# GpSimd takes layer-norm work, attention products are pre-added to two chunks, and the projections are re-ordered, in a fused attention and gated-MLP kernel

## Chip, cores and metric

The kernel runs on one core of a Trainium2 chip. The metric is the device time of that core in microseconds (us), the median of several executions. Every number below is such a time or comes from the profile of one execution. In the profile PE is TensorE, PEld its weight loads, DVE VectorE, ACT ScalarE, POOL GpSimd and SP SyncE, whose queue issues most transfers. "L371" is line 371 of the program. The changed kernel has one more line early on and three more in the middle, so L370 of before is L371 of after, L423 is L424, L545 is L548, L550 is L553, L576 is L579, and L607 is L610.

## The reference

```python
# S = 2048 tokens, D = 640, 32 heads of 20, F = 1536; bf16 inputs and outputs
xn  = layernorm(x)
q, k, v = split(xn @ wqkv)
# each token attends to 8 keys: itself and those 2, 4, ... 14 tokens back
logits = einsum("bhsd,bhswd->bhsw", q, k[gathered]) * 20 ** -0.5      # masked before token 0
attn   = softmax(logits)
o      = einsum("bhsw,bhswd->bhsd", attn, v[gathered])
out    = x + o @ wo + ((xn @ w_gate) * (xn @ w_up)) @ w_down
```

## The kernel before

A helper records every operation in program order and works out the semaphore waits from what each one reads and writes. Each engine then executes its own operations **in that recorded order**. An operation that waits holds up everything behind it on its engine: in the changed kernel's profile a copy that needs none of them stands behind 13.0 us of GpSimd's operations, and ScalarE stands 17.0 us for that copy.

Layer norm works on 16 tiles of 128 tokens. VectorE makes the statistics and the normalised tile. From tile 4 on, a transposing DMA writes the tile into `XNT`, which all projections read:

```python
def ln_apply(t):
    # ... cut
    op("dve", lambda e: e.reciprocal(rstd, sd), ...)
    op("dve", lambda e: e.tensor_scalar(xs, x, mv[:, 0:1], rstd, op0=ALU.subtract, op1=ALU.mult), ...)
    if t >= NTP:                                   # NTP = 4
        o = XNT[:, :, t * TS:(t + 1) * TS]
        op("sp", lambda e: e.dma_start_transpose(o, xs), ...)
```

Tokens are handled in two halves of 1024 (h = 0, 1), and in four blocks of 512 (j = 0 to 3) for the matmuls. The second half's keys need the last 14 keys of the first half, which GpSimd copies. This copy is the *seam*:

```python
def k_seam():
    o, i = KH[1][:, :, 0:PAD], KH[0][:, :, HS:HS + PAD]
    op("pool", lambda e: e.tensor_copy(o, i), r=[i], w=[o], name="kseam")
```

The logits are made without batched matmuls. VectorE multiplies q by shifted k for two offsets at a time (a *pair*; 4 pairs in each half). It works on five chunks of 128 channels: 3 into a slot of a ring (`SL`) and 2 into `TMP`. It then adds `TMP` to two of the three. TensorE sums what remains over the head channels with a 0/1 matrix, chunk by chunk:

```python
NKC = 3; NSL = 3
return [
    (..., prod(kept, 0, NKC)),              # 128 x 6144
    (..., prod(tmp, NKC, NCH)),             # 128 x 4096
    (..., lambda: op("dve", lambda e: e.tensor_tensor(a, a, b, ALU.add), ...)),   # 128 x 4096, 5 chunks -> 3
]
```

After the softmax, 16 copies for each half bring the weights into place (`ATB`), half of them issued on the SP queue and half on ScalarE's queue. Then eight *value products* of 256 tokens each follow on VectorE (`pv_steps`: a multiply of 128 x 10240, then three adds; the last add writes `VO`).

All other TensorE work is kept in a list in a fixed order: second-half q/k projections, v projections, gate and up matmuls, down projections. The generator keeps two running estimates, `t_pe` and `t_dve`. Each time it records a VectorE step it hands out TensorE work until `t_pe` has caught up:

```python
for i, (m, j, which) in enumerate([(m, j, which) for m in range(NCH) for j in (2, 3) for which in (0, 1)]):
    fill.append((1.08, lambda which=which, m=m, j=j: proj(which, m, j)))
# ... cut: v projections; then gate/up of blocks 0, 1; down of 0; gate/up 2; down 1; gate/up 3; down 2, 3

def run_fill(until, upto=None):
    # ... cut
        if it[0] == "dn":                 # a down-projection tile; it[1] = value product that it needs
            if pv_done[0] <= it[1]:
                return
    # ... cut

def tail(t, nb):       # one half (320 columns) of a down-projection tile: 12 matmuls with WD,
    # ... cut          # 5 with WO and VO, then the residual add FOUT on VectorE
```

Of the kernel before, what the change touches and what calls it, by code (L numbers as in the profile page):

```python
# [5 lines left out]
FP16 = mybir.dt.float16  # L6
ACT = mybir.ActivationFunctionType
ALU = mybir.AluOpType
# [3 lines left out]
NCH = 5  # L12
# [4 lines left out]
W = 8  # L17
# [11 lines left out]
HS = S // 2  # L29
SB = 256  # L30
NSB = HS // SB
# [181 lines left out]
def build_kernel(nc, A_x, A_wqkv, A_wo, B_x, B_w_gate, B_w_up, B_w_down, out):  # L213
    K = Sched(nc)
    op = K.op

    place = [16512]

    def sb(name, shape, dtype=BF16, at=None):
        n = mybir.dt.size(dtype)  # L220
        for s in shape[1:]:
            n *= s
        n = (n + 63) // 64 * 64
        if at is None:
            at = place[0]
            place[0] += n
        assert at + n <= 229344, (name, at + n)
        return K.sbuf(name, shape, dtype, at)
# [1 line left out]
    WG = sb("WG", [128, NCH, F])  # L230
    WU = sb("WU", [128, NCH, F])
    a_pr = place[0]
    NKC = 3
    NSL = 3
    WD = sb("WD", [128, NF, D], at=a_pr)
    WO = sb("WO", [128, NCH, D], at=a_pr + NF * D * 2)
    SL = [sb(f"SL{s}", [128, 2, NKC, HS], FP16) for s in range(NSL)]
    PVB = sb("PVB", [128, NCH, W, SB], FP16, at=place[0] - 2 * NKC * HS * 2)
    TMP = sb("TMP", [128, 2, NCH - NKC, HS], FP16)
    XNT = sb("XNT", [128, NCH, S])  # L240
    VO = sb("VO", [128, NCH, VP + S])
# [20 lines left out]
    NTP = 4  # L262
# [19 lines left out]
    def dma(o, i, r=(), w=(), name="", eng="sp", group=None):  # L282
        return op(eng, lambda e: e.dma_start(o, i), r=r, w=w, dma=True, name=name, group=group)  # L283
# [7 lines left out]
       r=[IDENT[:]], w=[IDENT[:]], name="ident")  # L291
# [3 lines left out]
       r=[G[:]], w=[G[:]], name="g1")  # L295
    op("pool", lambda e: e.affine_select(G[:], G[:], pattern=[[-4, H]], compare_op=ALU.is_ge,
                                         fill=0.0, base=0, channel_multiplier=1),
       r=[G[:]], w=[G[:]], name="g2")
# [3 lines left out]
    def x_load(t, eng="sp"):  # L302
        dma(XST[:, t % NXS, :], xhbm[t * TS:(t + 1) * TS, :], w=[XST[:, t % NXS, :]], name=f"xld{t}", eng=eng)
# [22 lines left out]
    def late_loads():  # L326
        wqkv_load(2)
        for T, src in ((WG, B_w_gate), (WU, B_w_up)):
            dma(T[:], src.rearrange("(c p) n -> p c n", p=128), w=[T[:]], name="ld_w")

    def down_loads():
        dma(WD[:], B_w_down.rearrange("(c p) n -> p c n", p=128), w=[WD[:]], name="ld_wd")

    def out_loads():
        dma(WO[:], A_wo.rearrange("(i m) n -> i m n", m=NCH), w=[WO[:]], name="ld_wo")
# [28 lines left out]
    def ln_apply(t):  # L364
        if t >= NT:
            return
        x, xs, mv = XST[:, t % NXS, :], XNS[:, t % NXN, :], MV[:, t, 0:2]
        sd, rstd = SD[:, t, 0:1], SD[:, t, 1:2]
        op("dve", lambda e: e.reciprocal(rstd, sd), r=[("sd", t)], w=[("rstd", t)], name=f"rstd{t}")  # L369
        op("dve", lambda e: e.tensor_scalar(xs, x, mv[:, 0:1], rstd, op0=ALU.subtract, op1=ALU.mult),  # L370
           r=[x, mv, ("rstd", t)], w=[xs], name=f"lnap{t}")  # L371
        if t >= NTP:
            o = XNT[:, :, t * TS:(t + 1) * TS]
            op("sp", lambda e: e.dma_start_transpose(o, xs), r=[xs], w=[o], dma=True, name=f"xT{t}")
        if t + 8 < NT:
            x_load(t + 8)
        elif t == NT - 1:
            late_loads()
# [26 lines left out]
    bank_ring = list(range(6))  # L405

    def bank():
        b = bank_ring.pop(0)
        bank_ring.append(b)
        return b  # L410
# [46 lines left out]
    def qk_steps(h, p, s):  # L457
        kept, tmp = SL[s], TMP
        kp = KH[h][:, 0, 0:1].ap[0]

        def prod(o, c0, c1):
            q = QH[h][:, c0:c1, :]
            k = KH[h][:, c0:c1, 4 * p:4 * p + HS + 2]
            kw = bass.AP(k.tensor, k.offset, [kp, [2, 2], [KL, c1 - c0], [1, HS]])
            qw = q.unsqueeze(1).to_broadcast([128, 2, c1 - c0, HS])
            return lambda: op("dve", lambda e: e.tensor_tensor(o[:], qw, kw, ALU.mult), r=[q, k], w=[o[:]],  # L466
                              name=f"prod{h}_{p}_{c0}")

        a, b = kept[:, :, 0:NCH - NKC, :], tmp[:]
        return [  # L470
            (0.16 + 2 * NKC * HS / 1920, prod(kept, 0, NKC)),
            (0.16 + 2 * (NCH - NKC) * HS / 1920, prod(tmp, NKC, NCH)),
            (0.16 + 2 * (NCH - NKC) * HS / 1920,
             lambda: op("dve", lambda e: e.tensor_tensor(a, a, b, ALU.add), r=[a, b], w=[a], name=f"psum{h}_{p}")),  # L474
        ]

    def qk_logits(h, batch):
# [49 lines left out]
        return head, rest  # L527

    def attn_move(h):
        for q in range(NSB):  # L530
            for r in range(4):
                src, dst = LOG[h][32 * q:32 * q + 32], ATB[h][r:128:4, q]
                dma(dst, src, r=[src], w=[dst], name=f"atb{h}_{q}_{r}", eng=("sp", "act")[r % 2], group=("atb", h))

    def pv_steps(b):
        h, q = divmod(b, NSB)
# [7 lines left out]
        def add(o, x, y, name):  # L544
            return lambda: op("dve", lambda e: e.tensor_tensor(o, x, y, ALU.add), r=[x, y], w=[o], name=f"{name}_{b}")  # L545

        P4, P2 = PVB[:, :, 0:4], PVB[:, :, 0:2]
        return [  # L548
            (0.16 + NCH * W * SB / 1920,
             lambda: op("dve", lambda e: e.tensor_tensor(PVB[:], vw, aw, ALU.mult), r=[v, a], w=[PVB[:]], name=f"pv_{b}")),  # L550
            (0.16 + NCH * 4 * SB / 1920, add(P4, P4, PVB[:, :, 4:8], "pa4")),
            (0.16 + NCH * 2 * SB / 1920, add(P2, P2, PVB[:, :, 2:4], "pa2")),
            (0.16 + NCH * SB / 1920, add(o, PVB[:, :, 0], PVB[:, :, 1], "pa1")),  # L553
        ]
# [1 line left out]

    pair_ctr = [0]
    h_pending = []
    h_keep = [1]

    def flush_h(keep):
        n = 0
# [79 lines left out]
    def tr(t):  # L642
        if t > 1:
            ln_next(t + 1)
        ln_pe(t)
        ln_copy(t)
        if t == 1:
            ln_next(t + 1)
# [9 lines left out]

    for t0 in (0, 2):
        bm = None  # L660
        for which in (0, 1):
            for t in (t0, t0 + 1):
                b = bank()
                proj_part(which, t, (0, 1), b, 0)
                if (which, t) == (1, 1):
                    tr(3)
                proj_part(which, t, (2, 3), b, 2 * TS)
                if (which, t) == (0, 0):
                    tr(1)
                part_evac(which, t, 1, 0, 4, b, 0)  # L670
                if bm is None:
                    bm = bank()
                proj_part(which, t, (4,), bm, (2 * which + t - t0) * TS)
                if (which, t) == (0, 1):
                    tr(2)
                if t >= 2 or (which, t) == (1, 1):
                    ln_step()
        for which in (0, 1):
            part_evac(which, t0, 2, 4, 1, bm, 2 * which * TS)
    bank_ring[:0] = [6, 7]  # L680
    for t0 in (4, 6):
        for g in range(5):
            b = bank()
# [5 lines left out]
            else:  # L689
                which, m = ((0, 0), (0, 2), None, (1, 0), (1, 2))[g]  # L690
# [7 lines left out]
    def exp_preload():  # L698
        op("act", lambda e: e.activation(DUM[:, 0:1], EPSC[:, 0:1], ACT.Exp), r=[EPSC[:]], w=[DUM[:]], name="exp_preload")

    t_pe, t_dve = [30.6], [31.5]
    fill, pos = [], [0]
    pv_done = [0]
    batches = []

    for i, (m, j, which) in enumerate([(m, j, which) for m in range(NCH) for j in (2, 3) for which in (0, 1)]):
        fill.append((1.08, lambda which=which, m=m, j=j: proj(which, m, j)))
        if i == 4:
            fill.append((0.0, exp_preload))
# [25 lines left out]
    def take():  # L735
        h, batch, at = batches.pop(0)
        qk_logits(h, batch)
        t_pe[0] = max(t_pe[0], at) + 0.44 + 0.2175 * NKC * len(batch)

    def run_fill(until, upto=None):  # L740
        while t_pe[0] < until and pos[0] < len(fill):
            if batches and t_pe[0] >= batches[0][2]:
                take()
                continue
            it = fill[pos[0]]
            if it[0] == "dn":
                if pv_done[0] <= it[1]:
                    return
                t_pe[0] += it[2]
                t_dve[0] += 0.48  # L750
                it[3]()
            else:
                t_pe[0] += it[0]
                d = it[1]()
                t_dve[0] += d if isinstance(d, float) else 0.0
            pos[0] += 1
        while batches and (t_pe[0] >= batches[0][2] or until >= batches[0][2]):
            take()
# [5 lines left out]
    def step(it):  # L764
        it[1]()
        t_dve[0] += it[0]
        run_fill(t_dve[0])

    slot = [0]

    def pair(h, p):
        s = slot[0] % NSL
        slot[0] += 1
        assert all(s != x for _, ps, _ in batches for _, x in ps)
        for it in qk_steps(h, p, s):
            step(it)
        return p, s
# [33 lines left out]
    headB, restB = softmax_steps(1)  # L811
    pv(0)
    settle()
    down_loads()
    out_loads()
    for it in headB:
        step(it)
    bank_ring[:] = bank_ring + [6, 7]
# [44 lines left out]
```

## Time and profile before

| | before |
|---|---|
| time, median of 4 | 267.12 us (266.22 to 268.76) |
| span of the profiled run | 265.8 us, mean granted clock 1.000 |
| TensorE busy | 256.7 us, 97% |
| VectorE busy | 215.7 us, 81% |
| ScalarE busy | 106.1 us, 40% |
| GpSimd busy | 5.3 us, 2% |

From the page of before: busy time of each engine, then the span in 40 slices of 6.6 us. A digit is tenths of busy time, and the PEclk row is the granted TensorE clock.

```profile
PE 256.7 (97%) x1669; PEld 151.2 (57%) x1669; DVE 215.7 (81%) x240; ACT 106.1 (40%) x193; POOL 5.3 (2%) x13
PE   8999979999999995999999999999999999999996
DVE  5799889999985992999997897999999999722211
POOL 2000050000100000000000000000000000000000
PEclk9999999999999999999999999999999999999999
```

TensorE is full, except for a small dip in the sixth slice and a larger one in the sixteenth. GpSimd is nearly unused. The list of waits of TensorE names every hole (engine and line, what it waited for, then total us, times, longest):

```profile
PE PS L576 <- ACT HT L578: 3.3, 1, 3.3
PE PS L423 <- DMA XNT<-XNS: 1.8, 1, 1.8
PE PS L401 <- DVE EPSC L287: 1.1, 1, 1.1
PE PS L436 <- ACT KH L450: 0.5, 1, 0.5
```

The 3.3 us: ScalarE issues eight attention copies (9.0 us) and in that time evacuates no bank. The 1.8 us: the second-half projections start with a channel group that needs the last tile of both blocks. The 1.1 us is the start of the program. So at most 5.6 us of TensorE's waiting could be removed. Anything more had to come from less TensorE work.

One stretch of VectorE's timeline, around the second value product (start, duration, line, operation; the idle time ahead of it in brackets):

```profile
132.50 5.48 DVE L550 TENSOR_TENSOR PVB<-VO,ATB 128x10240 f16<-128x10240 bf16 x1
140.09 0.49 DVE L611 TENSOR_TENSOR FOUT<-PS,XR 128x320 bf16<-128x320 f32 x1 [1.10 <-PE PS L607]
...
147.42 0.82 DVE L545 TENSOR_TENSOR VO<-PVB 128x1280 bf16<-128x1280 f16 x1
```

The second product is ahead of the first residual add of the down projection. Down projection tile 2, which needs that product, comes about 9 us after tile 0. The product is done just in time.

### The profile page before, as it was taken

The numbers are of one execution on the slowest core, as the hardware profiler recorded it, in microseconds if no ns is written. First come the engines' busy times: TensorE is split into PE (matmuls) and PEld (weight loads), VectorE is DVE, ScalarE is ACT, GpSimd is POOL, SyncE is SP. The second block draws the span as 40 slices with busy tenths as digits, with TensorE's granted clock in tenths as the row PEclk, the third lists the DMA queues.
The fourth block names the chain that finished last, engine by engine and source line by source line (L and its number), as shares of the span: only waits on it lengthen the run. The fifth ranks groups of instructions, "written<-read, shape, count | busy, mean of one in ns | idle before, by whom it ended". The sixth has DMA issues, their size and how long they took to land.

```text
span 265.8 us, 4020 instructions
## 1 busy us (share of the span) xinstructions
PE 256.7 (97%) x1669; PEld 151.2 (57%) x1669; DVE 215.7 (81%) x240; ACT 106.1 (40%) x193; POOL 5.3 (2%) x13
## 2 busy tenths in 40 slices
PE   8999979999999995999999999999999999999996
PEld 3899835455554442444457754446774444777775
DVE  5799889999985992999997897999999999722211
ACT  3565557555557514655560004752003555100000
POOL 2000050000000000000000000000000000000000
PEclk9999999999999999999999999999999999999999
DMA  6959689200000078009101189100113000031301
GB/s 197 322 131 148 122 257 403 83 2 0 0 0 2 0 157 232 3 7 357 57 0 49 52 175 206 36 2 0 49 52 100 0 0 2 4 94 52 99 27 49
DMA packets 21922, 23.46 MB, mean 88 GB/s; under 512 B 9872, under 2 KB 19472, under 8 KB 21904
## 3 DMA queue, kind: packets, MB, share of 16 engines
q1 hardware_dynamic: 20992, 20.95, 27.7%
q10 hardware_dynamic: 912, 2.26, 4.1%
q8 instruction: 13, 0.21, 0.3%
q14 instruction: 5, 0.04, 0.0%
HBM read 14.42 MB, written 2.62 MB: 64 GB/s over the span
## 4 chain that ended last, share of the span: by engine, by line
PE 82%; DVE 8%; ACTq 3%; DMA 3%; SPq 2%; issue 1%; ACT 1%
PE PS L576 37%; PE PS L607 28%; PE PS L423 16%; ACTq L283 3%; DVE XNS L370 2%; PE PS L484 2%; SPq L283 2%; DVE STATS L354 2%; DMA XST<-in_A_x_dram 2%; DVE STATS L348 2%; DMA XNT<-XNS 1%; DVE MV L360 1%; DVE SD L369 1%; ACT HT L578 0%; ACT USX L578 0%
## 5 line engine op out<-in xcount | busy, mean ns | idle before, releaser
L576 PE MATMUL PS<-XNT,WG 128*128 128x512 bf16 x240 | 59.7, 379 | 3.3 <-ACT HT L578 3.3
L576 PE MATMUL PS<-XNT,WU 128*128 128x512 bf16 x240 | 59.6, 379 | 0.0
L607 PE MATMUL PS<-WD,HT 128*128 128x320 bf16 (+1 forms) x396 | 57.6, 295 | 0.0
L578 ACT ACTIVATE HT<-PS 128x512 bf16<-128x512 f32 x48 | 29.1, 606 | 68.0 <-PE PS L576 34.5
L607 PEld LDWEIGHTS PS<-WD,HT 128*128 128x128 bf16 x396 | 38.1, 98 | 14.7
L423 PE MATMUL PS<-XNT,WQKV 128*128 128x512 bf16 x200 | 43.9, 379 | 1.8 <-DMA XNT<-XNS 1.8
L550 DVE TENSOR_TENSOR PVB<-VO,ATB 128x10240 f16<-128x10240 bf16 x8 | 43.9, 5486 | 0.1
L576 PEld LDWEIGHTS PS<-XNT,WG 128*128 128x128 bf16 x240 | 23.3, 98 | 31.7 <-ACT HT L578 3.8
L576 PEld LDWEIGHTS PS<-XNT,WU 128*128 128x128 bf16 x240 | 23.4, 98 | 28.5 <-issue 0.4
L611 DVE TENSOR_TENSOR FOUT<-PS,XR 128x320 bf16<-128x320 f32 (+1 forms) x33 | 15.5, 476 | 29.1 <-PE PS L607 29.1
L578 ACT ACTIVATE USX<-PS 128x512 bf16<-128x512 f32 x48 | 29.0, 605 | 17.7 <-PE PS L576 17.2
L423 PEld LDWEIGHTS PS<-XNT,WQKV 128*128 128x128 bf16 x200 | 23.3, 118 | 22.0 <-DMA XNT<-XNS 2.3
L545 DVE TENSOR_TENSOR PVB<-PVB 128x5120 f16<-128x5120 f16 (+1 forms) x16 | 34.4, 2148 | 0.0
L466 DVE TENSOR_TENSOR SL<-QH,KH 128x6144 f16<-128x6144 bf16 x8 | 26.8, 3352 | 1.4 <-ACT KH L450 1.4
L581 DVE TENSOR_TENSOR HT<-HT,USX 128x512 bf16<-128x512 bf16 x48 | 18.7, 416 | 10.9 <-ACT USX L578 10.9
L607 PE MATMUL PS<-WO,VO 128*128 128x320 bf16 (+1 forms) x165 | 27.1, 295 | 0.0
L607 PEld LDWEIGHTS PS<-WO,VO 128*128 128x128 bf16 x165 | 15.9, 98 | 5.9
L474 DVE TENSOR_TENSOR SL<-SL,TMP 128x4096 f16<-128x4096 f16 x8 | 18.3, 2289 | 0.2
L466 DVE TENSOR_TENSOR TMP<-QH,KH 128x4096 f16<-128x4096 bf16 x8 | 18.4, 2300 | 0.0
L429 ACT ACTIVATE VO<-PS 128x512 bf16<-128x512 f32 x20 | 11.9, 597 | 9.8 <-PE PS L423 9.8
L436 PE MATMUL PS<-XNT,WQKV 128*128 128x128 bf16 x200 | 12.7, 220 | 0.7 <-ACT KH L450 0.5
L436 PEld LDWEIGHTS PS<-XNT,WQKV 128*128 128x128 bf16 x200 | 11.6, 118 | 1.9 <-ACT KH L450 0.6
(49 smaller groups left out, 138.0 us busy)
## 6 DMA issues: line engine op xcount, KB each, us to landing
XR<-in_A_x_dram SPq DMA_DIRECT2D x16, 160.0 KB, 2.3
XST<-in_A_x_dram SPq DMA_DIRECT2D x15, 160.0 KB, 4.0
out_dram<-FOUT SPq DMA_DIRECT2D x15, 160.0 KB, 1.8
ATB<-LOG SPq DMA_DIRECT2D x16, 128.0 KB, 4.9
ATB<-LOG ACTq DMA_DIRECT2D x16, 128.0 KB, 5.0
WG<-in_B_w_gate_dram SPq DMA_DIRECT2D x1, 1920.0 KB, 9.9
WU<-in_B_w_up_dram SPq DMA_DIRECT2D x1, 1920.0 KB, 14.1
WD<-in_B_w_down_dram SPq DMA_DIRECT2D x1, 1920.0 KB, 8.3
```

The lines of the kernel that those rows point to most:

```text
L283: return op(eng, lambda e: e.dma_start(o, i), r=r, w=w, dma=True, name=name, group=group)
L423: op("pe", (lambda l, x, c: lambda e: e.matmul(PS[:, b, :], l, x, start=(c == 0), stop=(c == NCH - 1)))(l, x, c), r=[l, x], w=[PS[:, b, :] ...
L436: op("pe", (lambda o, l, x, st, sp: lambda e: e.matmul(o, l, x, start=st, stop=sp))(o, l, x, st, sp), r=[l, x], w=[o], name=f"pp{which}_{m ...
L466: return lambda: op("dve", lambda e: e.tensor_tensor(o[:], qw, kw, ALU.mult), r=[q, k], w=[o[:]], name=f"prod{h}_{p}_{c0}")
L474: lambda: op("dve", lambda e: e.tensor_tensor(a, a, b, ALU.add), r=[a, b], w=[a], name=f"psum{h}_{p}")),
L545: return lambda: op("dve", lambda e: e.tensor_tensor(o, x, y, ALU.add), r=[x, y], w=[o], name=f"{name}_{b}")
L550: lambda: op("dve", lambda e: e.tensor_tensor(PVB[:], vw, aw, ALU.mult), r=[v, a], w=[PVB[:]], name=f"pv_{b}")),
L576: op("pe", (lambda l, x, c: lambda e: e.matmul(PS[:, b, :], l, x, start=(c == 0), stop=(c == NCH - 1)))(l, x, c), r=[l, x], w=[PS[:, b, :] ...
L578: op("act", lambda e: e.activation(o, PS[:, b, :], ACT.Copy), r=[PS[:, b, :]], w=[o], name=f"guev{which}_{m}_{j}")
L581: h_pending.append(lambda: op("dve", lambda e: e.tensor_tensor(h, h, o, ALU.mult), r=[h, o], w=[h], name=f"h{m}_{j}"))
L607: op("pe", (lambda l, x, i, b: lambda e: e.matmul(PS[:, b, 0:wid], l, x, start=(i == 0), stop=(i == n - 1)))(l, x, i, b), r=[l, x], w=[PS[ ...
L611: op("dve", (lambda o, xr, b: lambda e: e.tensor_tensor(o, PS[:, b, 0:wid], xr, ALU.add))(o, xr, b), r=[PS[:, b, :], xr], w=[o], name=f"fi ...
```

## The change

Its intent was to relieve VectorE (12 normalisations go to GpSimd), to cut TensorE's logit matmuls from 96 to 64 (products added down from 5 chunks to 2 instead of 3), and to remove the three holes. Second-half projections go block by block, the attention copies leave ScalarE's queue, and the PSUM banks are taken in another order. With more slots in the ring, VectorE may run further ahead. The down weights then have to load later, after the last logits.

```diff
-    NKC = 3
-    NSL = 3
+    NKC = 2
+    NSL = 4
...
-        op("dve", lambda e: e.tensor_scalar(xs, x, mv[:, 0:1], rstd, op0=ALU.subtract, op1=ALU.mult),
+        op("dve" if t < NTP else "pool",
+           lambda e: e.tensor_scalar(xs, x, mv[:, 0:1], rstd, op0=ALU.subtract, op1=ALU.mult),
...
-            (0.16 + 2 * (NCH - NKC) * HS / 1920,
-             lambda: op("dve", lambda e: e.tensor_tensor(a, a, b, ALU.add), r=[a, b], w=[a], name=f"psum{h}_{p}")),
+            (0.16 + 4 * HS / 1920, add(kept[:, :, 0:2, :], tmp[:, :, 0:2, :])),
+            (0.16 + 2 * HS / 1920, add(kept[:, :, 0, :], tmp[:, :, 2, :])),
...
-        for q in range(NSB):
-            for r in range(4):
+        for r in range(4):
+            for q in range(NSB):
-                dma(dst, src, ..., eng=("sp", "act")[r % 2], group=("atb", h))
+                dma(dst, src, ..., group=("atb", h))
...
-    h_keep = [1]
+    h_keep = [3]
...
+        if t0 == 2:
+            bank_ring[:] = [5, 6, 0, 7, 2, 3, 4, 1]
-    bank_ring[:0] = [6, 7]
...
-    t_pe, t_dve = [30.6], [31.5]
+    t_pe, t_dve = [31.0], [31.8]
-    for i, (m, j, which) in enumerate([(m, j, which) for m in range(NCH) for j in (2, 3) for which in (0, 1)]):
+    for i, (m, j, which) in enumerate([(m, j, which) for j in (2, 3) for m in range(NCH) for which in (0, 1)]):
...
+        if h == 1 and batch[-1][0] == 3:
+            down_loads()
+            out_loads()
+            loaded.append(True)
...
-                if pv_done[0] <= it[1]:
+                if pv_done[0] <= it[1] or not loaded:
...
-        s = slot[0] % NSL
+        s = (slot[0] + NSL - 1) % NSL
... (left out: a new address for PVB, and the place where the weights were loaded before)
```

More of the change, by code (lines that the diff above doesn't have):

```diff
@@ L237, in build_kernel @@
     SL = [sb(f"SL{s}", [128, 2, NKC, HS], FP16) for s in range(NSL)]
-    PVB = sb("PVB", [128, NCH, W, SB], FP16, at=place[0] - 2 * NKC * HS * 2)
+    PVB = sb("PVB", [128, NCH, W, SB], FP16, at=place[0] + 4 * (NCH - NKC) * HS - 2 * NCH * W * SB)
     TMP = sb("TMP", [128, 2, NCH - NKC, HS], FP16)
@@ L467, in prod, with add @@
                               name=f"prod{h}_{p}_{c0}")
-        a, b = kept[:, :, 0:NCH - NKC, :], tmp[:]
+        def add(a, b):
+            return lambda: op("dve", lambda e: e.tensor_tensor(a, a, b, ALU.add), r=[a, b], w=[a], name=f"psum{h}_{p}")
         return [
@@ L529, in attn_move @@
     def attn_move(h):
-        for q in range(NSB):
-            for r in range(4):
+        for r in range(4):
+            for q in range(NSB):
                 src, dst = LOG[h][32 * q:32 * q + 32], ATB[h][r:128:4, q]
-                dma(dst, src, r=[src], w=[dst], name=f"atb{h}_{q}_{r}", eng=("sp", "act")[r % 2], group=("atb", h))
+                dma(dst, src, r=[src], w=[dst], name=f"atb{h}_{q}_{r}", group=("atb", h))
     def pv_steps(b):
@@ L704, in build_kernel @@
     batches = []
-    for i, (m, j, which) in enumerate([(m, j, which) for m in range(NCH) for j in (2, 3) for which in (0, 1)]):
+    loaded = []
+    for i, (m, j, which) in enumerate([(m, j, which) for j in (2, 3) for m in range(NCH) for which in (0, 1)]):
         fill.append((1.08, lambda which=which, m=m, j=j: proj(which, m, j)))
@@ L813, in build_kernel @@
     settle()
-    down_loads()
-    out_loads()
     for it in headB:
```

## The prediction

> **What bounds the kernel now.** TensorE. The page gives it 97% of a 265.8 us span at full clock; the chain of waits puts 82% on it. The list of waits and TensorE's timeline show only three gaps after the start: 0.5 us at 15.5 (a bank waiting for ScalarE), 1.9 us at 33.3 (projection waits for the transposed copy of tile 15), 3.4 us at 100.3 (ScalarE issues eight attention copies, 9.0 us, and evacuates nothing). VectorE is 81% busy and nearly full from 34 to 230 us.
>
> **What the change removes.** The bank order removes 0.5 us. Projections by token block need only tiles 8 to 11 first, so tile 15 has ten more groups (10.8 us) to land: 1.9 us. Copies on the SP queue: 3.4 us. Logit matmuls fall from 96 to 64; 24 cost 1.41 us in the timeline, so 32 cost 1.9 us. Together 7.7 us, all on the critical path: TensorE reaches the down projection of token block 0 at about 130 us instead of 137.6.
>
> **What it adds.** VectorE: one add of 128x2048 for each of 8 pairs, about 1.22 us between the 1.48 us (2560) and 0.82 us (1280) adds of the trace, with a dependency 1.25 us: 10 us in all. It gives back 12 x 0.41 us of normalising, about 2 us of start, and most of the 3.9 and 4.9 us idles before HT products (three stay pending now). So VectorE reaches the first value product at 117 us, as before, with TensorE 8 us ahead. GpSimd: I estimate 0.7 to 1 us per tile (its 128x128 select took 0.29 us, 128x32 0.21 us)[...]. Off the path.
>
> **Where it costs.** Two new waits appear in the changed instruction order.
> 1. The down weights load after the last logits, now only 6 matmul groups (6.5 us) before the down projection; before it was 18. They landed in 8.3 us, the output weights in 9.8 us: TensorE waits about 2 us.
> 2. TensorE's order is down projection tiles 0, 1, 2, 3, without other work between. VectorE's order puts the second value product behind the last FOUT add of tile 1, and tile 2 needs that product's result. After tile 1: FOUT 0.49, the two softmax operations 1.5, value product and three adds 5.48 + 2.82 + 1.48 + 0.82: 12.6 us, less 1.6 us of WD matmuls of tile 2. TensorE idles about 11 us near 142 to 154. Before, that product started at 132.5 and finished 0.2 us before it was needed.
>
> After that TensorE is 5.7 us later than before; later value products keep up, with perhaps 0.7 us more where HT products queue behind adds at the third down projection.
>
> **Sum.** 267.1 - 7.7 + 2 + 11 + 0.7 = 273.1 us. Range 270 to 275.8. Chances: faster 0.03, same 0.35, slower 0.62.
>
> **What would show it.** No wait of the projection on the transposes; no ScalarE issue gap; logits 64 matmuls; GpSimd about 10 us busy; TensorE reaching the first WD matmul at 129 to 131 and waiting 1 to 3 us on the WD load; one wait of 10 to 12 us of L610 on VectorE's adds; then none over 1 us.
>
> **What would make it wrong.** A GpSimd normalisation of 2 us or more would delay the transposes and give back the early gain. If the weights land in 6.5 us, it is 271.

## The result, and the profile after

| | before | after |
|---|---|---|
| time, median of 4 | 267.12 us (266.22 to 268.76) | **293.62 us** (292.03 to 294.87) |
| span of the profiled run | 265.8 us | 293.1 us |
| mean granted clock in it | 1.000 | 0.959 |
| TensorE busy | 256.7 us, 97% | 259.5 us, 89% |
| VectorE busy | 215.7 us, 81% | 223.2 us, 76% |
| GpSimd busy | 5.3 us, 2% | 43.4 us, 15% |

The ratio of after to before is 1.0981 (95%: 1.09 to 1.1062). Ratios here and below are the mean time of one kernel's fast runs over that of the other's in the same rounds, so they are not quite the ratio of the medians quoted. All four runs of after count as fast runs, although their clock is below 1: the lower clock belongs to the kernel, as will be seen. The predicted range was 270.0 to 275.8 us, so the time lies 20.5 us above the prediction and well outside the range.

From the page of after:

```profile
PE 259.5 (89%) x1621; PEld 151.3 (52%) x1637; DVE 223.2 (76%) x236; ACT 108.4 (37%) x193; POOL 43.4 (15%) x25
PE   8969592399999999999979229999999999999996
DVE  5876599998915399999943972999589999998222
POOL 1199999500000000000000000000000000000000
PEclk9999979589999999999999859999999999999999
```

TensorE has two damaged stretches, one between 15 and 60 us and one near 170 us. In the first, GpSimd is full from the third slice to the seventh. The clock falls in both. The list of waits of TensorE in after:

```profile
PE PS L610 <- DVE VO L548: 11.1, 1, 11.1
PE PS L424 <- ACT KH L430: 10.3, 1, 10.3
PE PS L424 <- DMA XNT<-XNS: 3.4, 1, 3.4
PE PS L444 <- DMA XNT<-XNS: 2.5, 1, 2.5
PE PS L610 <- DMA WD<-in_B_w_down_dram: 1.5, 1, 1.5
```

The first and the last lines are the two waits that were predicted (11 us and 2 us). The three others, 16.2 us together, were not. All three go back to one group, the GpSimd normalisation. Its durations in after, beside those of the four tiles left on VectorE (ns: min/median/max, then first and last start in us):

```profile
L371 POOL TENSOR_SCALAR XNS<-XST,MV,SD x12: 2502/2507/7222, 13.6 to 50.6; 128x640 bf16<-128x640 bf16 x12
L371 DVE TENSOR_SCALAR XNS<-XST,MV,SD x4: 445/446/447, 4.8 to 11.9; 128x640 bf16<-128x640 bf16 x4
```

GpSimd takes 2.51 us for what VectorE does in 0.45 us, and up to 7.2 us for one tile. The chain of waits of after shows the path (start, duration, what):

```profile
30.99 2.52 POOL XNS L371
33.52 2.63 DMA XNT<-XNS
36.19 4.29 issue
40.48 13.00 POOL XNS L371 x3
53.48 1.76 POOL KH L455
55.32 0.61 ACT KH L430
55.97 5.89 PE PS L424 x15
```

Tile 11 is ready at 33.5, and its transposed copy lands 2.6 us later, so the first second-half projection starts at 36.46 instead of 31.09. Tiles 13 to 15 take 13 us more. Behind them, in GpSimd's own order, stands the seam copy, which depends on none of these tiles. ScalarE's evacuation of the next keys was recorded after the seam and waits for it. In ScalarE's timeline the idle time is in brackets:

```profile
55.32 0.60 ACT L430 ACTIVATE KH<-PS 128x512 bf16<-128x512 f32 x1 [16.98 <-POOL KH L455]
```

While ScalarE stands for 17 us, no PSUM bank comes free, and TensorE stops for 10.3 us after it has filled those it has. The clock falls as well. Stretches of after (from:to and its length in us, busy us and count for PE, PEld, DVE, ACT and POOL, then the granted clock, DMA share and GB/s):

```profile
38.00:40.00 2.00, 2.00 (x6) 0.66 (x5) 1.97 (x2) 0.34 (x1) 2.00 (x1) 0.50 0.00 0
52.00:60.00 8.00, 4.03 (x10) 1.49 (x11) 7.97 (x4) 4.65 (x9) 3.23 (x2) 0.50 0.67 195
```

In the half-clock stretches of this stage TensorE was busy for about 3.4 + 5.1 us. Its matmuls of 128x512 took twice as long there (10 in 4.03 us from 52 to 60, against 19 in 4.00 us from 62 to 66 at clock 1.00), so half of the busy time is lost: an estimate of 4.2 us. By landmarks after is 5.4 us behind at the first second-half projection, 17.0 at the first gate matmul (96.29 against 79.31), 14.4 at the first down projection (151.94 against 137.58), and 27.4 at the first gate matmul of block 2 (183.49 against 156.05); from there to the end it stays at 27.

The second damaged stretch, on VectorE:

```profile
161.67 0.49 DVE L614 TENSOR_TENSOR FOUT<-PS,XR 128x320 bf16<-128x320 f32 x1 [1.49 <-PE PS L610]
...
163.53 5.49 DVE L553 TENSOR_TENSOR PVB<-VO,ATB 128x10240 f16<-128x10240 bf16 x1
169.06 4.35 DVE L548 TENSOR_TENSOR PVB<-PVB 128x5120 f16<-128x5120 f16 x2
173.44 0.83 DVE L548 TENSOR_TENSOR VO<-PVB 128x1280 bf16<-128x1280 f16 x1
```

Here the value product starts only behind the fourth residual add (each tile has two), and VectorE idles before each of these adds (3.23, 1.82, 1.22 and 1.49 us): the engine with the work waits in order for the engine that will soon need it. This part of the prediction is as it was written.

### The profile page after: what moved, and what is told of

It is laid out like the page before. It is cut to its first block, busy times and chain, and to the rows that moved or that the text cites. A ratio compares the mean times of both kernels' runs of the same rounds, so it can differ in the third digit from the quotient of the medians.

```text
span 293.1 us, 3946 instructions
## 1 busy us (share of the span) xinstructions
PE 259.5 (89%) x1621; PEld 151.3 (52%) x1637; DVE 223.2 (76%) x236; ACT 108.4 (37%) x193; POOL 43.4 (15%) x25
## 4 chain that ended last, share of the span: by engine, by line
PE 72%; POOL 8%; issue 6%; DMA 6%; DVE 5%; SPq 2%; ACT 0%; DVEq 0%; ACTq 0%; POOLq 0%
PE PS L579 33%; PE PS L610 25%; PE PS L424 13%; POOL XNS L371 8%; DMA WO<-in_A_wo_dram 3%; SPq L283 2%; DVE PVB L553 2%; DVE PVB L548 1%; DMA XST<-in_A_x_dram 1%; PE PS L487 1%; DMA XNT<-XNS 1%; POOL KH L455 1%; DVE STATS L348 0%; DVE VO L548 0%; DVE FOUT L614 0%
## 5 line engine op out<-in xcount | busy, mean ns | idle before, releaser
L424 PE MATMUL PS<-XNT,WQKV 128*128 128x512 bf16 x195 | 47.4, 405 | 14.1 <-ACT KH L430 10.3
L610 PE MATMUL PS<-WD,HT 128*128 128x320 bf16 (+1 forms) x396 | 58.3, 297 | 1.5 <-DMA WD<-in_B_w_down_dram 1.5
L579 PE MATMUL PS<-XNT,WG 128*128 128x512 bf16 x231 | 58.0, 379 | 0.7 <-issue 0.2
L424 PEld LDWEIGHTS PS<-XNT,WQKV 128*128 128x128 bf16 x200 | 23.8, 121 | 37.5 <-ACT KH L430 10.8
L371 POOL TENSOR_SCALAR XNS<-XST,MV,SD 128x640 bf16<-128x640 bf16 x12 | 39.9, 3340 | 11.1 <-DVE SD L369 11.1
L610 PE MATMUL PS<-WO,VO 128*128 128x320 bf16 (+1 forms) x165 | 27.8, 300 | 11.2 <-DVE VO L548 11.1
L471 DVE TENSOR_TENSOR SL<-SL,TMP 128x4096 f16<-128x4096 f16 (+1 forms) x16 | 30.2, 1885 | 0.3
L467 DVE TENSOR_TENSOR TMP<-QH,KH 128x6144 f16<-128x6144 bf16 x8 | 26.9, 3356 | 0.0
L584 DVE TENSOR_TENSOR HT<-HT,USX 128x512 bf16<-128x512 bf16 x48 | 18.8, 416 | 9.9 <-ACT USX L581 9.9
L467 DVE TENSOR_TENSOR SL<-QH,KH 128x4096 f16<-128x4096 bf16 x8 | 18.3, 2284 | 3.7 <-ACT KH L451 2.6
L430 ACT ACTIVATE KH<-PS 128x512 bf16<-128x512 f32 x10 | 6.0, 596 | 20.3 <-POOL KH L455 17.0
## 6 DMA issues: line engine op xcount, KB each, us to landing
WU<-in_B_w_up_dram SPq DMA_DIRECT2D x1, 1920.0 KB, 13.7
```

The costliest lines, as they stand in the source:

```text
L424: op("pe", (lambda l, x, c: lambda e: e.matmul(PS[:, b, :], l, x, start=(c == 0), stop=(c == NCH - 1)))(l, x, c), r=[l, x], w=[PS[:, b, :] ...
L430: op("act", lambda e: e.activation(o, PS[:, b, :], ACT.Copy), r=[PS[:, b, :]], w=[o], name=f"pev{which}_{m}_{j}")
L467: return lambda: op("dve", lambda e: e.tensor_tensor(o[:], qw, kw, ALU.mult), r=[q, k], w=[o[:]], name=f"prod{h}_{p}_{c0}")
L471: return lambda: op("dve", lambda e: e.tensor_tensor(a, a, b, ALU.add), r=[a, b], w=[a], name=f"psum{h}_{p}")
L579: op("pe", (lambda l, x, c: lambda e: e.matmul(PS[:, b, :], l, x, start=(c == 0), stop=(c == NCH - 1)))(l, x, c), r=[l, x], w=[PS[:, b, :] ...
L584: h_pending.append(lambda: op("dve", lambda e: e.tensor_tensor(h, h, o, ALU.mult), r=[h, o], w=[h], name=f"h{m}_{j}"))
```

## The experiments

Theory A: the miss is GpSimd's rate for the two-step normalisation. It delays the transposes and the seam, and the clock follows. Rival B: the seam queued behind the normalisations is most of it, and the rate matters little. Rival C, so called in the expectations of e1 and e2: the added product adds and the new order cost most. Rival D, tested in e7: GpSimd's operations slow VectorE's beside them, so the cost is in VectorE. Each edit is shown against after or before, as said. In the rounds of the experiments before had medians of 268.25 to 268.45 us.

### e1: normalise on VectorE again (against after)

```diff
-        op("dve" if t < NTP else "pool",
+        op("dve",
```

> The changed kernel with all sixteen normalisations on VectorE again; nothing else undone. Theory A (GpSimd at 2.5 us a tile[...] delays the transposes and the seam copy): the waits of 2.5, 3.4 and 10.3 us before 56 us and the half clock behind them go, about 18 to 20 us of the 26; the wait of 11 us on the second value product stays. Total 275 us (272 to 278). Rival C (the added product adds and the new order cost most): at most 6 us come back, 287 us or more.

276.01 us (275.21 to 278.74), ratio to before 1.032 (1.0244 to 1.0397). Moving this one operation back returns 17.6 of the 26.5 us, where rival C allowed 6 at most. The largest of TensorE's waits in it:

```profile
PE PS L610 <- DVE VO L548: 11.1, 1, 11.1
PE PS L610 <- DMA WD<-in_B_w_down_dram: 1.3, 1, 1.3
```

The three waits of the first stage are gone (what is left there is 0.3 us or less), and the first down-projection matmul comes at 131.8 instead of 151.9, where the prediction had it. The 11.1 us wait stays. During it the clock falls to half, and stays there until 159.9, though TensorE was busy again from 154.19: 5.7 us at half clock (12 matmuls with WD took 3.20 us in it, and 1.63 us right behind it), an estimate of 2.9 us lost. A stretch of it, in the columns used above:

```profile
148.00:157.00 9.00, 2.81 (x11) 1.64 (x12) 6.51 (x5) 0.00 (x0) 0.00 (x0) 0.50 0.00 0
```

### e2: only the GpSimd normalisation (against before)

```diff
-        op("dve", lambda e: e.tensor_scalar(xs, x, ...
+        op("dve" if t < NTP else "pool", lambda e: e.tensor_scalar(xs, x, ...
```

> The kernel before with only one part of the change: GpSimd normalises tiles 4 to 15. Theory A: this alone is enough for the loss; with its projections by output block the third group already needs tile 15, so TensorE stands from about 36 to 56 us: 290 us (286 to 296). Rival C: within 6 us of before, below 274 us.

296.59 us (294.95 to 298.09), ratio 1.1069 (1.0995 to 1.1144), just above the expected range: by itself this one move costs at least about as much as the whole change, since the two intervals overlap. Before's projection order needs tile 15 almost at once, so the wait is one piece:

```profile
PE PS L423 <- DMA XNT<-XNS: 23.9, 1, 23.9
```

In after, with its block-by-block order, the waits that go back to GpSimd come to 16.2 us. That the order softened the blow is read from these waits; no run isolates it.

### e3: the seam on ScalarE (against after)

```diff
-        op("pool", lambda e: e.tensor_copy(o, i), r=[i], w=[o], name="kseam")
+        op("act", lambda e: e.activation(o, i, ACT.Copy), r=[i], w=[o], name="kseam")
```

> The changed kernel with the seam copy on ScalarE, not behind the normalisations in GpSimd's queue. Theory A says that the projections of the last token block need tile 15 at nearly the time of the seam: TensorE gets through ten groups of the first block in place of seven, then waits for the transpose until 56 us: 290 us (288 to 292). Rival B (the harm comes only through the seam copy that queues behind the normalisations): the 10.3 us wait goes, 283 us or less.

290.75 us, ratio 1.0865 (1.0791 to 1.0939), 2.9 us better than after. Rival B falls. The wait for the seam turned into a wait for the tiles themselves:

```profile
PE PS L424 <- DMA XNT<-XNS: 8.2, 1, 8.2
PE PS L424 <- ACT KH L455: 1.7, 1, 1.7
```

The list of waits of after put 10.3 us on ScalarE. That wait was real, but another of 8.2 us, for the last tiles, lay hidden behind it.

### e4: GpSimd takes only tiles 4, 6, 8 and 10 (against after)

```diff
-        op("dve" if t < NTP else "pool",
+        op("pool" if t >= NTP and t % 2 == 0 and t < 12 else "dve",
```

> The changed kernel with GpSimd normalising only tiles 4, 6, 8 and 10, VectorE the others. One GpSimd tile of 2.5 us then spans two VectorE tiles, and GpSimd is done before the products start. Theory A: no wait on transposes over 1 us[...], about 274 us (271 to 277), a little below the run with all on VectorE. If GpSimd harms by any use of it, above 280 us.

277.87 us (276.91 to 279.56), ratio 1.0378 (1.0309 to 1.0448): my expectation was too low by 4 us. Even this light share lands on the path. Tile 4 takes 2.50 us instead of 0.45, and TensorE waits 2.46 us for the transposes (until 22.12), with a half-clock stretch behind it (granted clock 0.82 from 24 to 30). There is no slack for a slow first tile. Neither share of this operation that was tried on GpSimd (twelve tiles, four tiles) gained anything; that e4 is slower than e1 isn't clear of the noise.

### e5: e1 without the added pre-adding (against e1)

```diff
-    NKC = 2
-    NSL = 4
+    NKC = 3
+    NSL = 3
...
-            (0.16 + 4 * HS / 1920, add(kept[:, :, 0:2, :], tmp[:, :, 0:2, :])),
-            (0.16 + 2 * HS / 1920, add(kept[:, :, 0, :], tmp[:, :, 2, :])),
+            (0.16 + 2 * (NCH - NKC) * HS / 1920, add(kept[:, :, 0:NCH - NKC, :], tmp[:])),
...
-        s = (slot[0] + NSL - 1) % NSL
+        s = slot[0] % NSL
```

> The changed kernel with VectorE normalising and without the added product adds (three chunks kept, ring of three, as before). What remains of the change: bank order, projections by token block, copies on one queue, three pending HT products. If the added 10 us of VectorE work, through the instruction order that it gives, makes the two waits of e1_dve_norm (1.5 us on the down weights, 11.1 us on the second value product, 2 us of half clock behind it): both go, and the three gaps of the kernel before stay closed: 262 us (260 to 265). If the waits come from the other parts: 270 us or more.

262.11 us (261.9 to 262.26), ratio 0.9787 (0.9748 to 0.9825). The second value product starts at 122.77, ahead of the first residual add at 134.80, and after the start TensorE waits only 0.6 us. With the pre-adding (eight adds of 1.22 us in e1, 10 us in all) and its place in the generator's estimates, that product had been recorded behind the residual adds of tiles 0 and 1.

### e6: e1 with the second value product first (against e1)

```diff
-                if pv_done[0] <= it[1] or not loaded:
+                if pv_done[0] <= max(it[1], 1) or not loaded:
```

> e1_dve_norm with one rule of the order changed: no down-projection tile, and so no FOUT add, is placed before the second value product. If the 11 us come from VectorE's in-order place of that product behind the FOUT adds of tiles 0 and 1: the product starts about 11 us earlier, the wait and the half clock behind it go, 276 less 13 is 263 us (261 to 267). If VectorE simply has too much work by then: 270 us or more.

261.82 us (261.45 to 261.97), ratio 0.9772 (0.9726 to 0.9819). The second value product is now ahead of the residual adds on VectorE, and TensorE no longer waits for it:

```profile
131.72 5.48 DVE L553 TENSOR_TENSOR PVB<-VO,ATB 128x10240 f16<-128x10240 bf16 x1
143.37 1.68 DVE L614 TENSOR_TENSOR FOUT<-PS,XR 128x320 bf16<-128x320 f32 x4
```

All added adds are still there, no work is removed, and 14.2 us are gone against e1. So the 11.1 us wait was not a lack of VectorE time. It was the order. With it goes the half clock that followed it: granted clock 1.000 instead of 0.975.

### e7: twelve unread GpSimd operations in before

```diff
+            dd = FOUT[:, t % 2, :]
+            op("pool", lambda e: e.tensor_scalar(dd, XR[:, 0, :], mv[:, 0:1], rstd, op0=ALU.subtract, op1=ALU.mult),
+               r=[XR[:, 0, :], mv, ("rstd", t)], w=[dd], name=f"dead{t}")
...
(and the seam on ScalarE, as in e3)
```

> The kernel before, plus twelve GpSimd operations of the same form and size at the same points, whose results nobody reads (constant input, scratch output), and the seam copy on ScalarE. VectorE still normalises. Theory A (late results are the harm[...]): within 2 us of before, though VectorE loses 1 to 3 us where GpSimd operations run beside its products. [...]

Rival D's mark was 6 us or more slower.

Three fast runs of 267.88 to 270.19 us and one slow (273.06 us), which the ratio leaves out: 1.0044 (0.9984 to 1.0105), the same within the noise. The same GpSimd load, at the same points, with nobody waiting for the result, costs nothing that can be measured here (at most 1%), against 10.7% in e2. Rival D falls as an account of the miss. Each engine does lengthen the other's operations all the same. GpSimd's side and VectorE's side of it:

```profile
L375 POOL TENSOR_SCALAR FOUT<-XR,MV,SD x12: 2493/2587/8206, 13.7 to 58.1; 128x640 bf16<-128x640 bf16 x12
```

```profile
45.41 2.28 DVE L471 TENSOR_TENSOR TMP<-QH,KH 128x4096 f16<-128x4096 bf16 x1
47.73 2.69 DVE L479 TENSOR_TENSOR SL<-SL,TMP 128x4096 f16<-128x4096 f16 x1
```

A GpSimd operation that meets the products of a pair (5.6 us) lasts up to 8.2 us, while the products keep their time (2.28 us). The add behind them takes 2.69 us instead of 2.29 us; over the four adds beside GpSimd's operations (2.77, 2.69, 2.69 and 2.69 us) that is 1.7 us. (Spans on GpSimd are rough.)

### e8: which form is slow on GpSimd (before, with unread operations of six forms)

```diff
+            forms = (
+                lambda e: e.tensor_scalar(dd, sx, mv[:, 0:1], rstd, op0=ALU.subtract, op1=ALU.mult),
+                lambda e: e.tensor_copy(dd, sx),
+                lambda e: e.tensor_scalar(dd[:, 0:320], sx[:, 0:320], mv[:, 0:1], rstd, ...),
+                lambda e: e.tensor_scalar(dd, sx, 0.5, 2.0, op0=ALU.subtract, op1=ALU.mult),
+                lambda e: e.tensor_tensor(dd, sx, sx, ALU.add),
+                lambda e: e.tensor_scalar(dd, sx, rstd, None, op0=ALU.mult),
+            )
+            op("pool", forms[t % 6], ...)
```

> A look: the kernel before with twelve unread GpSimd operations of six forms (two-step with per-partition values at 640 and at 320 columns, two-step with constants, one-step with a per-partition value, copy, add of two tensors). If a cost per column makes the 2.5 us: 320 columns take about half, and the copy, which reads one tensor with no arithmetic, 0.8 us as I had estimated for the normalisation. If a fixed cost makes it: 320 columns take over 2 us.

One look, 273.1 us, state unknown, so only the durations are used. GpSimd's groups by form (busy us, then mean ns of one):

```profile
L376 POOL TENSOR_SCALAR FOUT<-XR,MV,SD 128x640 bf16<-128x640 bf16 x2 | 5.1, 2568 | 0.0
L381 POOL TENSOR_SCALAR FOUT<-XR,SD 128x640 bf16<-128x640 bf16 x2 | 4.1, 2056 | 1.6 <-DVE SD L370 1.6
L378 POOL TENSOR_SCALAR FOUT<-XR,MV,SD 128x320 bf16<-128x320 bf16 x2 | 3.2, 1585 | 0.0
L380 POOL TENSOR_TENSOR FOUT<-XR 128x640 bf16<-128x640 bf16 x2 | 2.6, 1295 | 10.3 <-DVE SD L370 10.3
L377 POOL COPY FOUT<-XR 128x640 bf16<-128x640 bf16 x2 | 1.4, 712 | 0.0
```

The two-step form costs 3.6 times a copy of the same tile. From its two widths, 320 columns cost 983 ns more, about 3.1 ns a column, with some 0.6 us fixed. One step instead of two saves only 0.5 us, and constants instead of per-partition values 0.2 us (2.35 us). An add of two such tiles took 1.30 us, half as long as the two-step form. My 0.7 to 1 us was the time of a copy.

### e12: after, with a plain copy on GpSimd (a wrong result)

```diff
-           lambda e: e.tensor_scalar(xs, x, mv[:, 0:1], rstd, op0=ALU.subtract, op1=ALU.mult),
+           (lambda e: e.tensor_scalar(xs, x, mv[:, 0:1], rstd, op0=ALU.subtract, op1=ALU.mult)) if t < NTP
+           else (lambda e: e.tensor_copy(xs, x)),
```

> The changed kernel with GpSimd's two-step normalisation of tiles 4 to 15 replaced by a plain copy (0.7 us in e8_pool_forms; the result is wrong on purpose). Engine, order and waits are the same; only the rate differs, and it is the one that I had estimated. If the rate alone made the miss: no wait on transposes over 1 us and none on the seam over 3 us, and the total is the predicted 273.1 plus the 2 us of half clock that follow the 11 us wait, 275 us (272 to 277). If it is the handing-over to GpSimd or its place in the order: 283 us or more.

274.79 us (274.06 to 275.86), ratio 1.0251 (1.0199 to 1.0304). The output is wrong (relative error 0.85). Engines, order, queues and waits are those of after; only the duration of twelve GpSimd operations differs:

```profile
L372 POOL COPY XNS<-XST 128x640 bf16<-128x640 bf16 x12 | 8.6, 720 | 18.6 <-DVE SD L369 14.8 <-DMA XNT<-XNS 2.8 <-DVE MV L360 1.1
```

TensorE's longest wait is the predicted one, and none is left on the transposes or the seam:

```profile
PE PS L611 <- DVE VO L549: 11.1, 1, 11.1
```

With the duration that I had assumed, the time falls into the predicted range. This settles that the miss was the size of that one term: of the 20.5 us, 18.8 go with it.

### e11: before with the attention copies on one queue

```diff
-        for q in range(NSB):
-            for r in range(4):
+        for r in range(4):
+            for q in range(NSB):
-                dma(dst, src, ..., eng=("sp", "act")[r % 2], group=("atb", h))
+                dma(dst, src, ..., group=("atb", h))
```

> The kernel before with one part of the change: attention copies all on the SP queue, row by row. The gap of 3.4 us at 100 us goes and VectorE's idle of 4.9 us beside it; the copies take about as long in all on one queue (10 us of issue for sixteen) as on two (9 us): 267.5 less 3.4 is 264 us (263 to 265.5). If one queue delays the first value product, 267 or more.

263.53 us (263.39 to 263.68), ratio 0.983 (0.9797 to 0.9863). The 3.3 us wait is gone, as the prediction said, and sixteen copies from one queue are issued in 10.15 us, against 6.85 us for eight on the SP queue and 9.00 us for eight on ScalarE's in before, or 9.8 us from the first issue to the end of the last. So two queues had saved only 0.3 us of issue time, and no engine waited for it here.

### e9: e5 and e6 together, with a later start assumed for VectorE (against e5)

```diff
-    t_pe, t_dve = [31.0], [31.8]
+    t_pe, t_dve = [31.0], [34.0]
...
-                if pv_done[0] <= it[1] or not loaded:
+                if pv_done[0] <= max(it[1], 1) or not loaded:
```

> e5_no_preadd with the value-product rule of e6_value_first, and the order's assumed start of VectorE moved from 31.8 to 34.0 us, where its products start when VectorE normalises. e5 had one wait of 0.6 us on logits left and none of the others, so little can come: 261.5 us (260.5 to 262.5). Slower than 263 would say that the later assumed start harms.

261.26 us (261.09 to 261.39, six runs), ratio 0.9745 (0.9716 to 0.9775): the lowest median of all, faster than both kernels, and correct. (Its interval overlaps those of e5 and e6, so that it beats them isn't shown.) Its only TensorE wait is the one of 1.1 us at the start.

### e10: e6 with a leaner time model in the generator (against e6)

```diff
-            (0.16 + 2 * NKC * HS / 1920, prod(kept, 0, NKC)),
+            (0.08 + 2 * NKC * HS / 1920, prod(kept, 0, NKC)),
... (the same in the three steps after it)
-    t_pe, t_dve = [31.0], [31.8]
+    t_pe, t_dve = [31.0], [33.4]
```

> e6_value_first with the order's assumed VectorE times nearer to the measured ones (0.08 instead of 0.16 us fixed in a product or add, start at 33.4), which puts the last logits, and so the load of the down weights, one pair of groups (2.2 us) earlier. The wait of 1.3 us on the weights and that of 0.6 us on logits go: 260 us (259 to 261.5), the best so far. If the weights still come late, 262.

262.52 us (261.43 to 263.81), ratio 0.9795 (0.9753 to 0.9837): a miss. The waits for the weights and the logits went away as expected, but a wait of 2.1 us for the second value product came in their place. Three runs had clock 1.0 (261.4 to 261.7 us) and three 0.993 (263.4 to 263.8). With pre-adding down to two chunks I got to 261.8 us, without it to 261.3 us. These two come from different rounds and differ in the assumed start as well, but the 32 saved matmuls bought nothing that could be shown: they take the logits' busy time on TensorE from 5.9 us (before) to 4.2 us (after), and they put 10 us on VectorE.

## Why the prediction was wrong

- **The failed step** is this: "GpSimd: I estimate 0.7 to 1 us per tile", with "Off the path" behind it. The tile took 2.51 us, and up to 7.2 us beside the attention products; twelve of them took 39.9 us instead of the "about 10 us busy" that I named as a sign. I scaled two selects (128x128 in 0.29 us, 128x32 in 0.21 us) as if any form took the time of its size; the estimate rested on nothing else that a trace showed. In e8 a copy of the tile does take about that (0.71 us), but a subtract-and-multiply with per-partition values 2.57 us. e1 and e12 show that this term makes nearly all of the miss: take it off GpSimd, 276.0 us; keep it there at a copy's speed, 274.8 us. What is left above 273.1 (2.9 and 1.7 us) is of the size of the half clock behind the 11 us wait, an estimated 2.9 us in each.
- **Why 2.5 us a tile was on the path.** Tiles 4 and up feed TensorE in order. Tile 11 was needed at about 31 us and ready only at 33.5 us, plus 2.6 us of landing. The last four, beside the products and their adds, came at 40.5 to 53.5 us. I had left this as a named risk ("2 us or more would delay the transposes and give back the early gain"), but gave it no time. It gave back not just the 7.7 us but 20 us: the waits of 2.5, 3.4 and 10.3 us, and an estimated 4.2 us of half clock, 20.4 us in all, against the 20.1 us by which after's first down projection lies behind that of e1.
- **What GpSimd meets beside VectorE's products.** In after the two tiles that start beside the products of a pair last 7.0 and 7.2 us instead of 2.5, and in e7 up to 8.2. Starting first did not help: in e7 the last one started at 58.1, 0.4 us ahead of the products at 58.53, and lasted 8.2 us, until 66.29. Beside the fp16 adds behind the products it is otherwise. In after both adds of the first pair run from 38.24 to 42.83 (4.59 us together, 2.29 and 1.22 us in e1, undisturbed), and tile 13 from 40.48 to 43.4: they overlap for 2.3 us, and that tile still takes only 2.9 us. There both engines grew, and neither stood still for long. Spans on GpSimd are rough, so this reading is less firm than the times; what makes the difference is not shown. The prediction had not costed any of this.
- **The seam** was not foreseen: I had read which engine runs an operation, and not what stands ahead of it there. Its share is small (e3: 2.9 us).
- **Right: the early gains.** With the normalisation back on VectorE there is no projection wait on transposes, no gap for copies, and the first down projection comes at 131.8 us after a wait of 1.3 us, so TensorE arrived at 130.5, inside the predicted 129 to 131. In after, the logit matmuls number 64 as said, and the weights cost 1.5 us of the predicted 2.
- **Right: the 11 us wait.** Predicted "about 11 us" from VectorE's order, measured 11.06 us in after, e1, e3, e4 and e12. e6 shows the mechanism: only the order changes, and it is gone.
- **Missing beside it: the clock.** None of my terms had a half clock behind the long wait. In after it held from about 166.8 to 177.1 and cost an estimated 1.4 us; in e1 an estimated 2.9 us, as much as lies between 273.1 and e1's 276.0. That match is partly luck, since before itself was 1.3 us slower in e1's rounds (268.38). The half clock is not equally long behind one and the same wait: 10.2 us behind the 11.1 us wait of after, as behind its 10.3 us wait, and 13.7 us in e1, so the cost varies by more than a microsecond. Nor does the length of a wait alone say whether it comes. In after 3.4 us of half clock followed the 3.4 us wait. As much followed waits of 2.29 us (e2) and 2.46 us (e4), and, by an estimate, one of 2.14 us (e3): in all three the 100 matmuls of 128x256 behind the wait took 12.78 us, against 11.11 us in after, where none followed a wait of 2.54 us. None followed the wait of 3.26 us in before's profiled run either. In after the mean clock was 0.959, and the half clock cost an estimated 5.6 us (4.2 and 1.4), 2% of the span. It also shows up as scatter between runs of one kernel: of 32 runs of before in the rounds of the experiments, which has one wait of 3.3 us, 10 had clock 1.000 (median 266.9 us), 19 had 0.993 to 0.994 (268.5 us), and three were lower still (269.7 to 273.3 us, two of them slow). All six of e11, where that wait is removed, had 0.999 or more and lie within 0.3 us. Three of six runs of e10, with a wait of 2.1 us, had 0.993 too; that the half clock lies behind that wait is argued, since its profiled run had 1.000.

What stays open: why GpSimd needs some 3 ns a column for the two-step form. No run here looks inside that operation. What sets off the half clock, and how long it holds, is open too: no run here varies the wait alone.

## What to carry to other kernels

An idle engine is not a free engine. Before moving an operation, find the duration of that very form and shape on the new engine, and if the trace has none, measure it alone first; then ask what waits for its result and what stands behind it in that engine's queue. When an engine waits for another that is itself partly idle, look at the order of instructions before removing work: here one changed condition returned 14 us with every operation kept. A TensorE wait can cost more than itself: here 1.4 to 2.9 us of half clock on top of one of 11 us and 1.7 us on top of one of 2.1 to 2.5 us, by estimates, and about 1.6 us in part of the runs with one of 3 us; behind one of 2.54 us, and one of 3.26 us in a profiled run, no half clock followed.
